# A gated spatial block behind linear attention: the written order of the work, who rounds ten pieces of W, and the unread products of the start

## The chip, the cores and the metric

The kernel runs on one core of a Trainium2 chip. The time is the device time of one execution in microseconds; of several executions the median counts. The profile shows one execution. The engines are TensorE (PE, with its weight loads PEld), VectorE (DVE), ScalarE (ACT), GpSimd (POOL) and SyncE (SP), which here only begins transfers.

## The reference

Linear attention with a product feature map, then a gated block whose gate mixes the positions:

```python
def phi(x):                                   # r = 8, so 64 features of 32 values
    a = np.einsum('rd,bhsd->bhsr', S1, x)
    b = np.einsum('rd,bhsd->bhsr', S2, x)
    return np.einsum('bhsi,bhsj->bhsij', a, b).reshape(*x.shape[:-1], r * r)
q_p, k_p = (phi(q), phi(k))                   # b, h, s, d = 4, 4, 1088, 32
kv = np.einsum('bhsf,bhsd->bhfd', k_p, v)
z = np.sum(k_p, axis=2)
num = np.einsum('bhsf,bhfd->bhsd', q_p, kv)
den = np.einsum('bhsf,bhf->bhs', q_p, z)[..., None] + 1e-06
x = num / den                                 # heads side by side: (4, 1088, 128)
h = np.maximum(x @ w_in, 0.0)                 # w_in (128, 1024)
u, v = (h[..., :512], h[..., 512:])
v_n = (v - mean(v)) / np.sqrt(var(v) + 1e-06)
v_s = np.einsum('ts,bsd->btd', w_spatial, v_n) + b_spatial[None, :, None]
return (u * v_s) @ w_out                      # w_out (512, 128)
```

S1, S2, w_in, w_out and w_spatial come as 64-bit or 32-bit numbers as they are drawn; the 64-bit ones are turned into 32-bit ones on the chip.

## The kernel before

Large products are made of three: each operand is split into a high part, rounded to the type fp32r, and a low part, the rest. `mm3` writes high x high, low x high and high x low into one bank. Small products of the attention (lines 759, 796, 845, 859, 873) use plain f32.

The names, with the batch as the first digit. `kab`, `qab`: projections of keys and queries with S1 and S2 (line 759); `ka`, `qa` copy one half out of the bank on ScalarE (764), `kp`, `qp` multiply the halves on VectorE (766). `kv0:1` to `kv0:3` sum keys x values (796); `kd0` masks that sum (822). `tq` turns the query features (845), `qpT` copies them (849), `nd` makes numerators and denominators (859), `x32` divides (866), `xt` turns x (873), `xh` and `xl` are its high and low parts (877, 878). `pv` is x times the second half of w_in (bank tag `sd`, two banks), in three pieces for each third of the positions; `vt` evicts it with relu (969), `st` and `mv` are its statistics (971, 972), `sd00` to `sd02` the square root (991), `t1`, `rs`, `nm` small steps behind it; `vt..:4` to `vt..:6` apply the norm (1007 on VectorE, 1010 on ScalarE), `vh` and `vl` are the parts of the result (1076, 1079). `pu` is the first half of w_in times x (bank `pu`, one bank), `u` its eviction (1127). `v9` holds rows of ones. `sp` are the products with W, w_spatial turned (1135 to 1146).

W comes in 9 rows of 128 positions (kt) and three column pieces c of 424, 332 and 332. `wt<kt><c>` is the load of a piece, `wTh` its rounding (line 732, on ScalarE), `wTl` its low part (736). The pieces c = 1 and 2 pass through seven buffers `pl`, those of c = 0 through `wl<kt>`. `wi_raw1`, `wi_raw0` and `wo_raw` are the halves of w_in and w_out as 64-bit numbers; `from_f64` turns them in seven steps (`wi_x1:1` to `wi_x1:7`, lines 655 to 668); `wih` and `wil` are the parts (672, 587).

The kernel is first recorded as a list of named operations and then laid out by `schedule`: a planner with costs for each operation. For batch 0 the list `ORDER` ranks all operations, and whichever engine is free takes the best-ranked operation that is ready by the planner's costs; for the rest the list `THEN` gives each engine's order. `FORCE` says on which engine some kinds run. An engine executes what it was given in that order and waits at the first instruction whose operands or buffer are not there. Where the planner sees TensorE idle it puts in products of zeros that nobody reads (`fill`, 64 columns, line 619); `small` makes groups of 32x32 products (606) at three places, and `N_WARM` = 5 warm products (600) stand at the start. A dummy square root on ScalarE, `eps:1` (line 625), is its first instruction.

Batch 0 has its attention alone in the head of the program, followed by pv and pu, and from then on the W products; the attentions of batches 1 to 3 lie among the main products of the batch ahead. In batch 3 the W products of part of the columns are made of sums of pieces (lines 1192 to 1385).

Of the kernel before, what the change touches and what calls it, by code (L numbers as in the profile page):

```python
# [70 lines left out]
ORDER = """  # L71
kt00:1 z9:1 eps:2 z9:2 s_raw:1 eps:1 v93:1 wps:1 v90:1 kt01:1 wps:2 v92:1 v91:1 wps:3 wi_raw1:1 wps:4
kt02:1 wps:5 qt00:1 wps:6 mask_sb:1 sk:1 sk:2 v00:1 sk:3 sk:4 b32:1 sk:5 sk:6 v01:1 sk:7 v02:1
kab00:1 kab01:1 ka00:1 kp00:1 ka01:1 kp01:1 ident_sb:1 wi_x1:1 qt01:1 wi_x1:2 kab02:1 wi_x1:3 ka02:1 wi_raw0:1 qab00:1 kp02:1
qt02:1 qa00:1 bh:1 kv0:1 wt10:1 wi_x1:4 wt70:1 kv0:2 qp00:1 wt00:1 wt50:1 kv0:3 wi_x1:5 wTl:10 tq00:1 bl:1
wi_x1:6 tq01:1 wt30:1 qpT00:1 qab01:1 kd0:1 qpT01:1 wi_x1:7 qa01:1 nd00:1 qp01:1 wih:1 wil:1 wt80:1 tq10:1 wi_x0:1
rec0:1 tq11:1 rec0:2 wt60:1 wi_x0:2 qab02:1 x320:1 qpT10:1 qpT11:1 qa02:1 wt40:1 wi_x0:3 wTh:2 xt0:1 qp02:1 nd01:1
xh0:1 wt01:1 wTh:8 xl0:1 wt11:1 wTh:1 wTl:2 pv000:1 rec1:1 wi_x0:4 wt21:1 wTh:6 pv001:1 wt20:1 rec1:2 vt00:1
wi_x0:5 wTl:11 tq20:1 x321:1 wTh:4 tq21:1 st000:1 vt00:2 wt31:1 xt1:1 qpT20:1 wi_x0:6 pv002:1 qpT21:1 wt41:1 wTl:6
wTh:9 nd02:1 wi_x0:7 xh0:2 wo_raw:1 wTh:7 xl0:2 wt51:1 wih:2 st001:1 pv010:1 wTh:10 rec2:1 vt00:3 wil:2 wTh:11  # L80
rec2:2 pv011:1 wTl:9 vt01:1 x322:1 qt10:1 qt11:1 pu000:1 wTh:12 qt12:1 vt01:2 st002:1 xt2:1 wt61:1 u000:1 st010:1
pv012:1 xh0:3 mv00:2 wTh:5 mv00:3 mv00:1 pu010:1 xl0:3 sd00:1 vt01:3 rs00:1 st011:1 pv020:1 u010:1 t100:1 wTh:3
st012:1 pv021:1 vt02:1 t100:2 mv01:2 pu020:1 rs00:2 mv01:1 vt02:2 nm00:1 mv01:3 vt00:4 pv022:1 sd01:1 u020:1 st020:1
vh00:1 pab10:1 st021:1 pu030:1 vt02:3 rs01:1 vl00:1 abT10:1 pab11:1 vt00:5 qd10:1 st022:1 pab12:1 wTh:16 sp000:1 qd10:2
mv02:1 t101:1 vh00:2 vt00:6 sp020:1 abT11:1 t101:2 sp010:1 vl00:2 vh00:3 qd11:1 sp030:1 mv02:2 wTh:14 rs01:2 sp000:2
mv02:3 qd11:2 nm01:1 vl00:3 wo_x:1 sp020:2 sp030:2 sd02:1 vt01:4 vt01:5 sp000:3 wTl:3 sp030:3 vh00:4 wo_x:2 sp010:2
vh00:5 vl00:4 sp020:3 sp010:3 wTh:13 rs02:1 wo_x:3 sp000:4 vt01:6 t102:1 vl00:5 sp010:4 wTh:15 sp030:4 t102:2 wTl:14
vh00:6 sp020:4 rs02:2 sp010:5 wo_x:4 wt71:1 abT12:1 sp030:5 qd12:1 nm02:1 vl00:6 sp020:5 vt02:4 sp000:5 qd12:2 vt02:5
sp000:6 vt02:6 vh00:7 sp030:6 vh00:8 sp010:6 vl00:7 sp020:6 vh00:9 vl00:8 sp030:7 v91:2 sp010:7 v92:2 vh00:10 wTh:17
sp030:8 v90:2 wTl:8 sp010:8 v93:2 sp000:7 wTl:1 sp030:9 sp000:8 wTl:5 sp020:7 wo_x:5 sp020:8 wTl:4 sp030:10 sp030:11  # L90
wo_x:6 sp030:12 sp020:9 sp020:10 wTl:13 sp020:11 kt10:1 sp020:12 wTl:7 sp010:9 kt11:1 sp010:10 sp010:11 wo_x:7 sp010:12 kt12:1
sp020:13 sp020:14 wTl:17 sp000:9 wt81:1 woh:1 sp000:10 sp000:11 wTl:16 wt02:1 sp000:12 sp000:13 wTl:15 sp000:14 wt12:1 sp000:15
wTl:12 sp000:16 wt22:1 sp000:17 wTl:18 sp000:18 sp010:13 wt32:1 wol:1 sp020:15 sp020:16 wt42:1 sp020:17 sp020:18 wTl:19 sp030:13
v10:1 sp030:14 u000:2 sp030:15 wt52:1 sp030:16 wTh:18 sp030:17 u020:2 kab10:1 g000:1 v11:1 wTl:20 wTh:19 v12:1 g000:2
wTh:20 wt62:1 sp001:1 wTl:21 ka10:1 kt20:1 wTh:21 sp001:2 ka11:1 u030:1 kt21:1 wTl:22 sp001:3 wTh:22 sp030:18 wt72:1
sp001:4 wTh:23 wTl:23 u030:2 pu001:1 wt82:1 sp001:5 wTl:25 u001:1 kt22:1 sp010:14 wTh:24 sp010:15 sp010:16 sp010:17 wTl:26
fa100:1 sp010:18 sp001:6 u010:2 sp011:1 fb100:2 wTl:24 g010:1 sp001:7 fb100:1 sp001:8 g010:2 sp001:9 fa101:1 sp011:2 u001:2
po00:1 gh001:1 po00:2 fb101:1 wTh:26 gl001:1 sp011:3 g020:1 sp011:4 wTh:27 g030:1 sp011:5
""".split()
# [1462 lines left out]
```

## Time and profile before

| | before |
|---|---|
| median of 3 executions | 324.55 us (324.24 to 326.92) |
| span of the profiled execution | 322.9 us |
| TensorE busy | 317.1 us, 98% |
| VectorE, ScalarE, GpSimd busy | 228.1, 165.2, 64.2 us |

The span goes from the first to the last instruction; 1.65 us of the median lie around it. Busy time of TensorE is from its records, whose ends are modelled, and unread products count in it. A row of the time order gives start, duration of the group, engine, line, operation, tiles and, in brackets, the idle time ahead of it and what ended that. A product of plain f32 makes two records, a transpose one.

### The profile page before, as it was taken

The numbers are of one execution on the slowest core, as the hardware profiler recorded it, in microseconds if no ns is written. First come the engines' busy times: TensorE is split into PE (matmuls) and PEld (weight loads), VectorE is DVE, ScalarE is ACT, GpSimd is POOL, SyncE is SP. The second block draws the span as 40 slices with busy tenths as digits, with TensorE's granted clock in tenths as the row PEclk, the third lists the DMA queues.
The fourth block names the chain that finished last, engine by engine and source line by source line (L and its number), as shares of the span: only waits on it lengthen the run. The fifth ranks groups of instructions, "written<-read, shape, count | busy, mean of one in ns | idle before, by whom it ended". The sixth has DMA issues, their size and how long they took to land.

```text
span 322.9 us, 6972 instructions
## 1 busy us (share of the span) xinstructions
PE 317.1 (98%) x2708; PEld 301.9 (93%) x2708; DVE 228.1 (71%) x512; ACT 165.2 (51%) x391; POOL 64.2 (20%) x81
## 2 busy tenths in 40 slices
PE   8999999999999999999999999999999999999995
PEld 7887998999999899999899999999999999999995
DVE  3999995647799972889875658896325688439382
ACT  3499935525774625566535567462414465416040
POOL 1000004557201035321004702250001321103000
PEclk9999999999999999999999999999999999999999
DMA  7874129563010375001044215001000421000001
GB/s 237 294 230 142 50 60 293 187 196 87 14 59 20 89 240 152 7 26 39 9 122 130 63 49 168 2 0 44 1 0 2 121 71 42 0 3 0 2 1 69
DMA packets 21549, 26.84 MB, mean 83 GB/s; under 512 B 2828, under 2 KB 21260, under 8 KB 21516
## 3 DMA queue, kind: packets, MB, share of 16 engines
q1 hardware_dynamic: 21516, 26.39, 26.4%
...
## 4 chain that ended last, share of the span: by engine, by line
PE 86%; ACT 6%; DVE 4%; DMA 1%; issue 1%
PE sp L1135 17%; PE sp L1137 14%; PE sp L1144 14%; PE sd L1369 4%; PE sp L1369 3%; PE sd L577 3%; PE sd L579 3%; PE sd L578 3%; PE pu L577 3%; PE po L577 2%; PE po L579 2%; PE po L578 2%; PE sp L1146 2%; PE pu L578 2%; PE pu L579 2%; ACT wTh L732 2%
## 5 line engine op out<-in xcount | busy, mean ns | idle before, releaser
L1135 PE MATMUL sp<-wTh,vh 128*128 128x332 f32 (+1 forms) x350 | 114.8, 328 | 0.0
L1137 PE MATMUL sp<-wTh,vl 128*128 128x332 f32 (+1 forms) x304 | 99.0, 326 | 0.0
L1135 PEld LDWEIGHTS sp<-wTh,vh 128*128 128x128 f32 x350 | 65.7, 188 | 2.1 <-issue 0.7
L1144 PE MATMUL sp<-wl,vh 128*128 128x332 f32 x192 | 59.8, 311 | 0.0
L1137 PEld LDWEIGHTS sp<-wTh,vl 128*128 128x128 f32 x304 | 57.1, 188 | 0.8
L1144 PE MATMUL sp<-wTl,vh 128*128 128x424 f32 x112 | 37.1, 349 | 0.0
L1144 PEld LDWEIGHTS sp<-wl,vh 128*128 128x128 f32 x192 | 36.0, 188 | 0.0
L672 ACT CAST g<-u 128x332 fp32r<-128x332 f32 (+1 forms) x41 | 19.8, 490 | 31.6 <-DVE u L1172 21.4
L587 DVE TENSOR_TENSOR g<-u,g 128x332 fp32r<-128x332 f32 (+1 forms) x41 | 23.4, 572 | 17.1 <-PE po L578 11.2
L1172 DVE TENSOR_TENSOR u<-sp,u 128x332 f32<-128x332 f32 (+1 forms) x43 | 22.4, 520 | 14.8 <-PE sp L1146 8.4
L945 DVE RECIPROCAL c<-c 128x384 f32<-128x384 f32 (+1 forms) x9 | 21.8, 2419 | 15.1 <-ACT c L943 15.1
L1127 ACT ACTIVATE u<-pu 128x332 f32<-128x332 f32 (+1 forms) x44 | 20.6, 468 | 20.8 <-PE pu L579 15.9
L1048 ACT CAST vh<-vt 128x384 fp32r<-128x384 f32 x36 | 17.4, 511 | 19.3 <-DVE vt L1007 10.7
L914 POOL TENSOR_TENSOR pl<-pl,pl 128x384 f32<-128x384 f32 (+1 forms) x18 | 17.9, 1005 | 42.1 <-DMA pl<-qd 41.7
L971 DVE BATCH_NORM_STATS2 st<-vt 128x6 f32<-128x512 f32 x36 | 24.0, 684 | 2.1 <-ACT vt L969 1.9
L969 ACT ACTIVATE vt<-sd 128x512 f32<-128x512 f32 x36 | 21.4, 604 | 7.3 <-PE sd L579 6.6
L590 POOL TENSOR_TENSOR r<-pl,r 128x384 fp32r<-128x384 f32 (+1 forms) x18 | 17.6, 984 | 34.5 <-ACT r L672 34.5
L1050 DVE TENSOR_TENSOR vl<-vt,vh 128x384 fp32r<-128x384 f32 (+1 forms) x36 | 18.4, 522 | 5.4 <-ACT vh L1048 5.2
L1144 PEld LDWEIGHTS sp<-wTl,vh 128*128 128x128 f32 x112 | 21.0, 188 | 0.1
L736 POOL TENSOR_TENSOR wl<-pl,wTh 128x332 fp32r<-128x332 f32 x8 | 7.0, 901 | 50.9 <-ACT wTh L732 50.9
L577 PE MATMUL pu<-xh,wih 128*128 128x332 f32 (+1 forms) x48 | 16.5, 345 | 0.3 <-ACT kp L1127 0.3
L1007 DVE TENSOR_SCALAR vt<-vt,mv,sm 128x512 f32<-128x512 f32 x32 | 16.4, 559 | 0.0
...
## 6 DMA issues: line engine op xcount, KB each, us to landing
...
```

Source lines behind the costliest of these rows:

```text
L577: nc.tensor.matmul(o, ah, bh, start=start, stop=False)
L578: nc.tensor.matmul(o, ah, bl, start=False, stop=False)
L579: nc.tensor.matmul(o, al, bh, start=False, stop=stop)
L587: return lambda: nc.vector.tensor_tensor(out=o(), in0=a(), in1=bb(), op=ALU.subtract)
L945: op("DVE", 135 + 6.3 * n, lambda x32=x32, n=n: nc.vector.reciprocal(out=x32[:, :n], in_=x32[:, :n]), w=[x32])
L969: op("ACT", c_act(512, True), lambda pv=pv, t=t: nc.scalar.activation(vt[:, t], pv.ap, AF.Relu), r=[pv], w=[(vt, t)])
L971: op("DVE", 690, lambda stats=stats, t=t: nc.vector.bn_stats(out=stats.ap, in_=vt[:, t]), r=[(vt, t)], w=[stats])
L1135: nc.tensor.matmul(sp[:, :cw], vh[:, kt], wTh[:, kt, cs], start=(kt == begin), stop=False)
L1137: nc.tensor.matmul(sp[:, :cw], vl[:, kt], wTh[:, kt, cs], start=False, stop=False)
L1144: nc.tensor.matmul(sp[:, :cw], vh[:, kt], w_lo(kt, c), start=False, stop=False)
L1172: op("DVE", c_dve(cw), lambda: nc.vector.tensor_tensor(out=u.ap, in0=sp[:, :cw], in1=u.ap, op=ALU.mult), r=[sp], w=[u], lead=LEAD[1])
L1369: nc.tensor.matmul(x[:, :cw], p, q, start=i == 0 and n == 0, stop=end and i == 3 and n == 2)
```

## The change

- `ORDER`, `THEN`, `FORCE` and the paces are replaced by one list `SEQ`, which names each of 1808 operations with its engine; each engine executes its names in that order. `schedule` only plays the lists through with costs, to choose buffers and to place the fills.
- `load_w` may have the high part rounded by a transfer from SBUF to SBUF that GpSimd begins (`wTh:n@POOL`, line 707 of the new file). The new program has ten of these.
- The last step of `from_f64` and the low parts of w_in and w_out may run on GpSimd. In the head these go from VectorE to GpSimd: wi_x1:7, wil:1, wi_x0:7, wil:2, three low parts of W and vl00:3; more do so later. Some norms go from VectorE to ScalarE, the first step of `from_f64` of wi_x1 and wo_x from ScalarE to VectorE.
- Eight warm products instead of five, no groups of small products, fills of 128 columns instead of 64, of which eight are in the program, all of them ahead of kab02.
- The order of the loads differs: wi_raw1 comes second. `eps:1` comes late in ScalarE's order.

```diff
-N_WARM = 5
-SMALL_AT = ("pv011:1", 22)
-SMALL_FILL = (12, 15)
-N_SMALL = 36
+N_WARM = 8
...
+s_raw:1@SP z9:1@DVE z9:2@DVE wi_raw1:1@SP v91:1@POOL wps:1@PE v90:1@POOL kt00:1@SP wps:2@PE wps:3@PE kt01:1@SP wps:4@PE v00:1@SP wps:5@PE mask_sb:1@SP
...
+    def schedule(self):
+        ops = self.ops
+        lists = {}
+        for x in SEQ:
+            name, e = x.split("@")
+            lists.setdefault(e, []).append(name)
...
-    def small(n=None, out=None):
-        out = out or wps
-        for i in range(n or N_SMALL):
-            q = 32 * (i % 4)
-            nc.tensor.matmul(out[q:q + 32, :32], z9[:, q:q + 32], z9[:, :32], start=True, stop=True, tile_position=(0, q))
-
-    op("PE", 1300, f4=True, fn=small, r=[z9], w=[wps], due=0)
...
-        filled.append(tag)
-        if len(filled) == SMALL_FILL[0]:
-            small(SMALL_FILL[1], homes[tag, slot])
-        else:
-            nc.tensor.matmul(homes[tag, slot][:, :64], z9.ap, z9[:, :64], start=True, stop=True)
+        nc.tensor.matmul(homes[tag, slot][:, :P], z9.ap, z9.ap, start=True, stop=True)
...
-        step(c1, lambda v: v.tensor_tensor(out=out() if out else x(), in0=x(), in1=ev(), op=ALU.add), [(x32, "e"), (x32, "x")], [w_out or (x32, "x")])
...
+        def add(v):
+            return lambda: v.tensor_tensor(out=out() if out else x(), in0=x(), in1=ev(), op=ALU.add)
+
+        op("DVE", c1, add(nc.vector), r=[(x32, "e"), (x32, "x")], w=[w_out or (x32, "x")], sh=True, alts=[("POOL", c_pool(n), add(nc.gpsimd))] if n > NSK else [])
...
-        op("ACT", c_act(cw), lambda: nc.scalar.copy(out=wTh[:, kt, cs], in_=raw[:, :cw]), r=[raw], w=[(wTh, (kt, c))])
+        cast = "POOL", C_SWD, lambda: nc.gpsimd.dma_start(out=wTh[:, kt, cs], in_=raw[:, :cw])
+        op("ACT", c_act(cw), lambda: nc.scalar.copy(out=wTh[:, kt, cs], in_=raw[:, :cw]), r=[raw], w=[(wTh, (kt, c))], kb=cw // 2, alts=[cast])
```

The start of TensorE's order before: warm and small products, a fill, two projections of keys, eight fills, the third projection, a projection of queries, the sums of keys and values.

```order
L600 MATMUL sd_161<-u_87 128x128 x5
L606 MATMUL sd_161<-u_87 32x32 x36
L619 MATMUL po_222<-u_87 128x64
L759 MATMUL sd_224<-sk,kt 64x2x32 x6
L759 MATMUL sd_161<-sk,kt 64x2x32 x6
L619 MATMUL po_222<-u_87 128x64 x8
L759 MATMUL sd_224<-sk,kt 64x2x32 x6
L759 MATMUL sd_161<-sk,c_124 64x2x32 x6
L619 MATMUL po_222<-u_87 128x64
L796 MATMUL pu_273<-v,kp_93 32x33 x24
L796 MATMUL pu_273<-v,kp_94 32x33 x24
L796 MATMUL pu_273<-v,kp_95 32x33 x24
```

And after, in the same place:

```order
L587 MATMUL sd_159<-u_87 128x128 x8
L592 MATMUL po_187<-u_87 128x128 x2
L735 MATMUL sd_190<-sk,kt 64x2x32 x6
L735 MATMUL sd_159<-sk,kt 64x2x32 x6
L592 MATMUL po_187<-u_87 128x128 x6
L735 MATMUL sd_190<-sk,kt 64x2x32 x6
L772 MATMUL pu_225<-v,kp_93 32x33 x24
L735 MATMUL sd_159<-sk,c_124 64x2x32 x6
L772 MATMUL pu_225<-v,kp_94 32x33 x24
L735 MATMUL sd_190<-sk,c_125 64x2x32 x6
L818 MATMUL po_187<-u_88,kp_93 128x128 x3
L818 MATMUL po_300<-u_88,kp_93 128x128 x3
L772 MATMUL pu_225<-v,kp_95 32x33 x24
```

The small products are gone, two of the fills come ahead of kab00 and six ahead of kab02, none comes behind, and the projections of queries stand between the sums.

ScalarE before, from the eviction vt00:3 (the first row, line 969) on; sd00 is the row of line 991.

```order
L969 ACTIVATE vt_92<-sd_224 128x512
L732 CAST wTh<-pl_148 128x332
L969 ACTIVATE vt_90<-sd_161 128x512
L732 CAST wTh<-pl_149 128x332
L969 ACTIVATE vt_90<-sd_224 128x512
L1127 ACTIVATE kp_93<-pu_273 128x424
L877 CAST xh_117<-sp_427 128x384
L732 CAST wTh<-wl_109 128x424
L991 ACTIVATE sm_71<-mv_80,eps 128x3
L969 ACTIVATE vt_90<-sd_161 128x512
L1127 ACTIVATE kp_94<-pu_273 128x424
```

And after, from vt00:3 to the xh of the last third:

```order
L937 ACTIVATE vt_92<-sd_190 128x512
L647 CAST wih<-v 128x512
L708 CAST wTh<-pl_148 128x332
L708 CAST wTh<-wl_109 128x424
L959 ACT_TABLE_LOAD
L959 ACTIVATE sm_71<-mv_80,eps 128x3
L937 ACTIVATE vt_90<-sd_159 128x512
L937 ACTIVATE vt_90<-sd_190 128x512
L708 CAST wTh<-wl_111 128x424
L850 CAST xh_117<-sp_376 128x384
L708 CAST wTh<-wl_101 128x424
L937 ACTIVATE vt_90<-sd_159 128x512
```

The square root has a table load ahead of it, and three of the evictions come behind it; there are fewer casts of W (line 732 before, 708 after) in between.

GpSimd before, behind its four casts at the start:

```order
L736 ISA
L736 TENSOR_TENSOR wl_782<-pl_145,wTh 128x332
L736 TENSOR_TENSOR wl_750<-pl_151,wTh 128x332
L736 TENSOR_TENSOR wl_678<-pl_150,wTh 128x332
L736 TENSOR_TENSOR wl_772<-pl_146,wTh 128x332
```

And after, from the first operation behind two of these casts:

```order
L641 TENSOR_TENSOR vt_91<-vt_91 128x512
L602 CAST v_137<-u_87 64x128
L602 CAST v_138<-u_87 64x128
L577 TENSOR_TENSOR wil<-vt_91,wih 128x512
L707 DMA wTh<-wl_103 128x424
L641 TENSOR_TENSOR v<-v 128x512
L712 TENSOR_TENSOR wTl_106<-wl_107,wTh 128x424
L577 TENSOR_TENSOR wil<-v,wih 128x512
L712 TENSOR_TENSOR wl_464<-pl_148,wTh 128x332
L707 DMA wTh<-wl_105 128x424
L707 DMA wTh<-pl_149 128x332
```

Before, low parts of the third column piece of W are all that stands there; after, the two halves of w_in (lines 641 and 577), the first transfers (707) and low parts of the first piece stand ahead.

## Rows read from the trace of the kernel before

**Rows 1.** The page: span, busy time of each engine, the chain by engine.

```profile
span 322.9 us, 6972 instructions
...
PE 317.1 (98%) x2708; PEld 301.9 (93%) x2708; DVE 228.1 (71%) x512; ACT 165.2 (51%) x391; POOL 64.2 (20%) x81
...
PE 86%; ACT 6%; DVE 4%; DMA 1%; issue 1%
```

**Rows 2.** Windows: us, busy time and count by engine, PEclk, DMA share, GB/s.

```profile
0.00:5.00 5.00, 3.68 (x83) 3.39 (x83) 1.68 (x10) 1.49 (x2) 1.21 (x8) 1.00 0.55 146
5.00:18.20 13.20, 12.58 (x307) 11.57 (x308) 11.27 (x23) 6.42 (x18) 0.00 (x0) 1.00 0.92 312
18.20:32.10 13.90, 13.90 (x122) 10.60 (x121) 13.82 (x40) 13.68 (x33) 0.00 (x0) 1.00 0.55 176
...
54.60:318.80 264.20, 264.01 (x2050) 254.76 (x2051) 180.67 (x391) 129.39 (x306) 61.66 (x72) 1.00 0.20 62
```

**Rows 3.** All waits of TensorE: us in total, times, longest.

```profile
PE sd L600 <- DVE u L596: 1.3, 1, 1.3
PE po L845 <- DVE kp L766: 0.6, 1, 0.6
PE pu L577 <- ACT kp L1127: 0.3, 1, 0.3
```

**Rows 4.** TensorE in order of time, 0 to 40 us.

```profile
1.32 2.50 PE L600 MATMUL sd<-u 128*128 128x128 f32 x10 [1.32 <-DVE u L596]
3.75 1.19 PE L606 MATMUL sd<-u 128*32 128x32 f32 x72
...
5.49 1.30 PE L759 MATMUL sd<-sk,kt 128*64 128x64 f32 x24
6.72 2.00 PE L619 MATMUL po<-u 128*128 128x64 f32 x16
8.65 0.57 PE L759 MATMUL sd<-sk,kt 128*64 128x64 f32 x12
...
12.02 0.88 PE L845 MATMUL po<-u,kp 128*128 128x128 f32 x6 [0.62 <-DVE kp L766]
...
13.59 1.50 PE L859 MATMUL sp<-u,c 128*128 128x66 f32 x12
...
18.21 0.48 PE L577 MATMUL sd<-wih,xh 128*128 128x512 f32 x1
...
19.68 0.82 PE L845 MATMUL po<-u,kp 128*128 128x128 f32 x6
...
23.61 0.60 PE L606 MATMUL po<-u 128*32 128x32 f32 x44
...
25.82 0.48 PE L577 MATMUL sd<-wih,xh 128*128 128x512 f32 x1
```

**Rows 5.** VectorE in order of time, 3 to 20 us.

```profile
10.41 0.68 DVE L661 SCALAR_TENSOR_TENSOR vt<-vt,vt 128x512 uint32<-128x512 uint32 x1
11.01 0.95 DVE L766 TENSOR_TENSOR kp<-ka,sd 128x768 f32<-128x768 f32 x1
...
14.61 0.69 DVE L587 TENSOR_TENSOR wil<-vt,wih 128x512 fp32r<-128x512 f32 x1
```

**Rows 6.** ScalarE in order of time, 0 to 35 us.

```profile
0.73 1.28 ACT L625 ACT_TABLE_LOAD   x1 [0.73 <-PEq L1550]
...
17.53 1.44 ACT L732 CAST wTh<-wl 128x424 fp32r<-128x424 f32 x3
```

**Rows 7.** GpSimd by line: count, busy us, mean ns.

```profile
L736 POOL TENSOR_TENSOR wl<-pl,wTh 128x332 fp32r<-128x332 f32 x8 | 7.0, 901 | 50.9 <-ACT wTh L732 50.9
```

**Rows 8.** The chain that ended last, in order of time.

```profile
31.45 0.71 ACT vt L1010
...
47.21 4.58 DMA pl<-in_wT
```

**Rows 9.** VectorE in order of time, 119 to 121.5 us.

```profile
120.45 1.45 DVE L587 TENSOR_TENSOR g<-u,g 128x424 fp32r<-128x424 f32 x1 [0.61 <-ACT g L672]
```

More of the change, by code (lines that the diff above doesn't have):

```diff
@@ L73 @@
[L73 to L92, printed above, removed]
@@ new lines @@
+kab02:1@PE kv0:1@PE ka02:1@ACT wi_raw0:1@SP wi_x1:5@DVE qab00:1@PE kp02:1@DVE wt10:1@SP qa00:1@ACT kv0:2@PE wt80:1@SP qp00:1@DVE qab01:1@PE qa01:1@ACT
+wi_x1:6@DVE bh:1@ACT tq00:1@PE tq01:1@PE qp01:1@DVE qpT00:1@ACT wi_x1:7@POOL kv0:3@PE qpT01:1@ACT qab02:1@PE kd0:1@DVE nd00:1@PE qa02:1@ACT wt01:1@SP
+v92:1@POOL wih:1@ACT qp02:1@DVE v93:1@POOL wt30:1@SP wi_x0:1@ACT wil:1@POOL wt11:1@SP tq10:1@PE rec0:1@DVE wt50:1@SP tq11:1@PE rec0:2@DVE x320:1@DVE
+qpT10:1@ACT wt20:1@SP tq20:1@PE qpT11:1@ACT wTh:2@POOL wi_x0:2@DVE wt40:1@SP xt0:1@PE nd01:1@PE wi_x0:3@DVE wt70:1@SP xh0:1@ACT wi_x0:4@DVE wt21:1@SP
@@ new lines @@
+wt31:1@SP xl0:1@DVE tq21:1@PE wt60:1@SP rec1:1@DVE wi_x0:5@DVE pv000:1@PE rec1:2@DVE wt41:1@SP x321:1@DVE qpT20:1@ACT wTh:9@ACT qpT21:1@ACT wTh:4@ACT
+pv001:1@PE wi_x0:6@DVE vt00:1@ACT wt00:1@SP xt1:1@PE st000:1@DVE wt51:1@SP wi_x0:7@POOL pv002:1@PE xh0:2@ACT vt00:2@ACT xl0:2@DVE nd02:1@PE
+wo_raw:1@SP vt00:3@ACT wTl:4@POOL st001:1@DVE wih:2@ACT st002:1@DVE wTh:11@ACT pv010:1@PE wil:2@POOL rec2:1@DVE wTh:5@ACT mv00:2@DVE rec2:2@DVE
+mv00:3@DVE mv00:1@DVE x322:1@DVE pv011:1@PE sd00:1@ACT vt01:1@ACT rs00:1@DVE wTl:2@DVE pu000:1@PE vt01:2@ACT t100:1@DVE st010:1@DVE wTl:13@POOL
@@ L248 @@
 class Op:
-    __slots__ = ("n", "name", "eng", "fn", "occ", "dur", "deps", "succ", "due", "left", "ready", "first", "tiles", "start", "end", "chosen", "alts", "kb", "rw", "stretch", "sh", "after", "f4")
+    __slots__ = ("n", "name", "eng", "fn", "deps", "succ", "left", "first", "tiles", "start", "end", "alts", "kb", "sh", "after", "f4")
 class Fill:
@@ new lines, in schedule @@
+            for e, os in lists.items():
+                if at[e] == len(os) or os[at[e]].left:
+                    continue
+                o = os[at[e]]
+                s = max([free[e], o.after, *(d.end + (-165 if d.eng == e == "PE" else self.LAT.get((d.eng, e), 35)) for d in o.deps)])
+                if e == "POOL":
+                    s = max(s, shared_to - 40)
+                need = {}
+                for t in o.first:
+                    if t.slot is None:
+                        need.setdefault(t.tag, []).append(t)
+                ok = True
+                for tag, ts in need.items():
+                    n = len(ts)
+                    if n > len(slots[tag]) or [t.n for t in ts] != list(range(taken[tag], taken[tag] + n)):
+                        ok = False
+                        break
+                    s = max(s, slots[tag][n - 1][0])
+                if ok and (best is None or s < best[0]):
+                    best = (s, e, o)
@@ L411, in schedule @@
                     order += [Fill(lambda home=home: self.fill(*home))] * n
[L412 to L418 removed]
+            o.start = s
             for t in o.first:
```

500 lines of the change are left out of this document (222 added, 278 removed).

## The prediction

> **What bounds the kernel now.** I read the page first. TensorE is busy for 317.1 us of a span of 322.9 us, and 86% of the chain that ended last is its own work [rows 1]. So the end moves only if TensorE gets less to do, does it in less time, or waits less. The windows show where that could be [rows 2]: from 54.6 to 318.8 us it is busy for 264.01 of 264.20 us, which leaves 0.19 us. All of its idle time that an operand ends is three waits, 1.3, 0.6 and 0.3 us [rows 3]; the first is the start of the program.
>
> The busy share hides one thing. In the first 24 us TensorE also runs products that nobody reads, and these are waiting time under another name. In time order [rows 4]: 2.50 us of warm products and 1.19 us of small ones before the first keys at 5.49, sixteen records of them at 6.72 that last until the next keys at 8.65, and 0.60 us of small ones at 23.61, in front of pv011. (Three pieces of 0.43 to 0.45 us between 9.5 and 16.6 us are not shown.) From kab00 on they come to 1.93 + 0.60 + three times some 0.44 = 3.85 us; with the waits of 0.6 and 0.3 us the head could give back 4.75 us at most.
>
> What sets the pace there are the other engines. From 5.0 to 18.2 us VectorE is busy for 11.27 of 13.20 us; from 18.2 to 32.1 us VectorE has 13.82 and ScalarE 13.68 of 13.90 us [rows 2]. TensorE's 13.90 of 13.90 us there is no proof that it sets the pace, since it holds small products and pipelined ends. All the gain to be had lies before some 55 us.
>
> **The early gaps.** Eight warm products take the place of five and of the 36 small ones. A warm product is two records; ten took 2.50 us, the next work starting 2.43 us after the first, so eight take 8 x 0.49 = 3.9 us and end at 5.2 us (before: warm and small ended at 4.94). Two of the new 128-column products follow. One of 64 columns took 0.24 us at 6.72 (1.93 us for eight, two records each); six transposes of 128 columns at 19.68 took 0.82 us, 0.14 us a record, so two records of the new width are 0.27 us. I take 0.24; by the warm ones it would be 0.49, and kab02 below would come 2 us later. kab00 can start at 5.7 us, against 5.49. Its data no longer lead the queue: 512 KB of wi_raw1 stand ahead of them. By 5.0 us 146 GB/s had brought 730 KB [rows 2], and s_raw, wi_raw1 and kt00 are 768 KB, so the load is late by 0.1 to 0.5 us at most against 5.2 us and TensorE would not get there sooner anyhow. Two projections (1.3 us) and six fills (1.45 us) put kab02 at 8.4 us, against 8.65: 0.2 us, hardly a gain.
>
> The gain comes behind it, on VectorE. Now a step of from_f64 (started 0.60 us ahead) stands between kp02 and qp00 [rows 5]; with wi_raw1 early it is done before, so qp00 starts 0.2 + 0.60 = 0.8 us earlier, and what follows from it in a line (tq00, now at 12.02 after the wait of 0.62 us, then kd0 and, at 13.59, nd00) does too. kd0 has one step of from_f64 and the second qp ahead of it on VectorE, 0.68 + 0.95 us; that takes qp00's end at 11.15 to 12.8 us and leaves 0.2 to 0.8 us for nd00. Between nd00 and pv000 stood wi_x1:7 and wil:1, some 0.69 us each, both of which go to GpSimd, so the shorter gain grows again. I take 0.8 us at pv000 (18.21 before, 17.4 now); bounds 0.2 and 1.4.
>
> **From pv000 to the W products.** TensorE loses work in this stretch: tq20 and tq21 (0.82 us) now lie before pv000, and the 0.60 us of small products are gone. By TensorE alone pv022 ends 0.8 + 0.8 + 0.6 = 2.2 us earlier. By ScalarE it is less. Up to the last of the nine evictions (vt) it has six casts of W to do in place of twelve: 6 x 0.48 = 2.9 us less [rows 6]. Against that stand one ACT_TABLE_LOAD of 1.28 us and up to two norms of 0.71 us each [rows 8], which VectorE did before. The balance is between 1.6 us less and 0.2 us more, 0.7 us less in the middle; with the earlier start that is 0.8 + 0.7 = 1.5 us. The smaller of the two counts, so **1.5 us**, bounds 0.6 and 2.2.
>
> The table load has to be placed. Before, the dummy square root is ScalarE's first instruction and its load lies at 0.73 us, where nothing waits. Now that dummy comes after 75 rows, and the load that the square root needs stands in front of sd00, with the evictions vt01:1 and vt01:2 queued behind it. These free the two banks which pv012 and pv020 write; in between TensorE has pu000, xt2 and the product before, some 1.6 us by the distance from the end of the small products at 24.21 to pv012 at 25.82 [rows 4]. The wait is thus partly covered; uncovered it is 1.3 us, and my 1.5 us becomes 0.6.
> The load's 1.28 us [rows 6] agree with 1283 ns in the Trainium skill, "ScalarE: Activation LUTs", section "What ACT_TABLE_LOAD costs"; that page adds a drain of some 1.38 us to each switch, which no row here shows, since nothing ran ahead of the load. By it the sum would be worse by up to 1.4 us.
>
> **wil:2 on GpSimd.** pu000 reads it as the third of its three products. wi_x0:7, wih:2, one low part of W and wil:2 follow each other there. GpSimd did 332 columns in 901 ns [rows 7], so 512 columns are 1.4 us if that grows in proportion, against 0.69 us on VectorE [rows 5]. The two operations cost 1.4 us more in a row, but VectorE is freed of some 2.7 us ahead of wi_x0:6. I take 0; bounds 0 and 0.7 us.
>
> **The transfers that GpSimd begins.** The built program has ten of them, not eleven. Eight of them stand in GpSimd's list ahead of the second round of v92, in the stretch that ends at some 50 us. Each takes a cast of 0.48 us from ScalarE, and I have no row of a transfer that GpSimd begins. The nearest is the load of a W slice by SP, which ScalarE waited 4.58 us for [rows 8]; that was mostly a wait for its buffer and for the transfers ahead. The low part of W has to wait for such a transfer, on VectorE in most cases. I take 0, because wTh:2 comes right behind wil:1, near 15 us, and the first W product stands at 32; bounds -0.3 and +4.6 us. The casts behind it ended in TensorE's last wait of 0.3 us [rows 3]; the order there is another, and I count **0.3 us** gained, bounds 0 and 0.3.
>
> **Behind 55 us.** TensorE has the same products to do in another order: 0 for that, +-0.3. VectorE and GpSimd get more in common. Where a two-input VectorE operation meets GpSimd's, it took 1.45 us for 424 columns [rows 9], where 512 columns had taken 0.69: at least 0.76 us more. GpSimd's rows grow from 86 to 138. VectorE idles for 83 of the 264 us, so most of this is absorbed; I take +0.3 us, bounds 0 and 2.
>
> **The sum.** -1.5 - 0.3 + 0.3 = -1.5 us on a profiled span of 322.9 us, so 321.4 us. The median is 324.55, with 1.65 us around the span; these stay. Forecast: **323.0 us**. Its own range, from 2.2 + 0.3 gained to the cover of the table load gone and the low bounds elsewhere, is 321.5 to 325.0.
>
> **The rivals.**
> *The head gives back nearly all of it.* If VectorE and ScalarE, freed of some 4 us each, let TensorE run through, most of the 4.75 us go: 4 of them make 320.5 us. For it: the two engines are full in just this stretch. Against it: the eight unread products at 6.7 us wait for keys that now come later, and these 1.9 us stay. It decides where pv000 starts before 16.5 us. Faster by over 1% is below 321.3 us, about what a measurement of this kernel can tell from no change. Chance 0.25.
>
> *GpSimd becomes late.* Up to 50 us it gets five operations of 512 columns at 1.4 us, three low parts at 0.9 to 1.15 us and eight transfers. If each of these has to wait for a VectorE operation to end (VectorE is 85 to 99% busy in the two windows before 32 us), it runs at the pace of collisions as in [rows 9], double its own: 10.2 us of operations become 20, and the transfers queue behind them. wil:2 would then come 2 us late, and the last high parts of W's second columns some 3 us after their products are due; TensorE's list is fixed, so it has nothing to do in their place. 2 + 3 - 1.5 = +3.5 us: **328.0 us**, slower. It decides when wTh:10 lands after 50 us. Against it: VectorE's operations from PSUM or in place are many, and GpSimd sat idle to 53 us.
> A rule speaks for this rival: the Trainium skill, "SBUF — State Buffer", section "Who interferes with whom", has a transfer begun by GpSimd starved of its descriptors while VectorE runs in a two-port mode, and names another queue as the cure. No row of before shows such a transfer. Chance 0.11.
>
> *The clock.* All small products and all fills behind kab02 are gone. The granted clock reads 1.00 in every window [rows 2], the 2.4 GHz level; still the first products, after idleness, took 0.24 us a record where the transposes of that width at 19.68 took 0.14. If the level fell to 1.2 GHz between 9 and 18 us, the products on the path there (three projections, four transposes, nd00, xt0: some 4.5 us) would take that again: 323.0 + 4.5 = 327.5. It decides if PEclk reads below 1.00 there. Against it: TensorE has real work in most of that time. Chance 0.05.
>
> *Nothing comes through.* TensorE's work from 18 us on is the bound and the new orders only move waits: 324.5 us. It shares the band with the forecast; the two hold 0.59.
>
> **How the numbers follow.** Faster 0.27 (the first rival and the forecast's lower edge), same 0.59, slower 0.14 (GpSimd 0.11, part of the clock). Below 320.3 and above 327.3 lie some 0.1 each, so the range is 320.3 to 327.3.
>
> **What the profile after would show.** kab02 near 8.4, nd00 near 13, pv000 at 17.0 to 18; no unread product after 9 us; a load of 1.28 us on ScalarE near 22 us, and behind it a wait of TensorE on vt01 below 1.3 us; the first W product (32.10 before) at 30.6; no wait of 0.3 us near 54; TensorE waits below 0.5 us behind. I am wrong if TensorE waits for GpSimd's parts, if the W products start after 32 us, or if the gain at 32 us is lost between 32 and 55 us.

## The result

The new kernel takes **328.79 us** (median of 4, 327.85 to 329.62) against 324.39 (4 runs): ratio 1.0137, interval 1.0103 to 1.0172. It is slower by 1.4%, clear of the noise; the forecast was 323.0 us, and the range ended at 327.3. The profiled span is 327.0 us, 4.1 more than before (322.9), so the loss is inside the span. Medians count every execution; ratios leave out those in a slow state, over 1.5% above the fastest of their kernel.

The page after, its head and the row of the granted clock ([rows 1] before):

```profile
span 327.0 us, 6708 instructions
...
PE 318.4 (97%) x2562; PEld 302.4 (92%) x2562; DVE 218.6 (67%) x470; ACT 164.4 (50%) x382; POOL 105.2 (32%) x133
...
PEclk9999899999999999999999999999999999999999
```

TensorE's work is nearly the same; the span is longer by waits and, in this execution, by a slice in which the clock reads 8. GpSimd's busy time rises from 64.2 to 105.2 us, VectorE's falls by 9.5 us, ScalarE's hardly.

TensorE's waits (total, times, longest; [rows 3] before):

```profile
PE sd L566 <- ACT vt L937: 2.3, 2, 1.8
...
PE pu L772 <- issue: 0.6, 1, 0.6
PE sd L566 <- ACT xh L850: 0.3, 1, 0.3
PE po L818 <- DVE kp L742: 0.3, 1, 0.3
```

Windows, columns as in [rows 2]:

```profile
18.20:32.10 13.90, 11.24 (x58) 8.55 (x58) 12.62 (x33) 11.78 (x25) 7.14 (x8) 0.96 0.72 230
32.10:54.60 22.50, 22.50 (x119) 20.63 (x118) 17.79 (x46) 14.38 (x30) 7.69 (x11) 0.95 0.39 106
54.60:318.80 264.20, 263.94 (x2080) 254.44 (x2079) 173.05 (x357) 130.60 (x311) 85.71 (x103) 1.00 0.23 68
```

Where before TensorE had no idle time from 18.2 to 32.1 us, it now has 2.66, and PEclk is below 1.00 there and in the next window. From 54.6 us on nothing is lost: TensorE idles there for 0.26 us, before for 0.19. To say where the 4 us arise, I counted at which time TensorE had begun the same number of columns of products that are read in the two traces (warm products, small ones and fills left out, 666,432 columns in all; the order differs, so single points can mislead by some 0.5 us). The last column is an experiment further down:

```
columns begun   before, us   after minus before   both edits minus before
     18,000         21.0            +0.3                  +0.3
     24,000         25.7            -0.5                  -0.5
     27,000         27.2            +1.0                  -0.2
     29,000         27.9            +3.3                  +0.8
     30,000         28.4            +3.7                  +0.8
     33,000         30.1            +4.8                  +0.9
     47,000         36.9            +4.5                  +1.5
     90,000         57.2            +3.4                  +0.4
    660,000        316.0            +4.0                  +0.9
```

At 25.7 us the new kernel is 0.5 us ahead (the small products at 23.61 are gone), and then more than 5 us are lost by 30 us. TensorE in order of time there and ahead of it ([rows 4] before):

```profile
8.96 0.57 PE L735 MATMUL sd<-sk,kt 128*64 128x64 f32 x12
...
11.91 0.87 PE L818 MATMUL po<-u,kp 128*128 128x128 f32 x6 [0.27 <-DVE kp L742]
...
13.72 0.39 PE L772 MATMUL pu<-v,kp 128*32 128x33 f32 x21 [0.56 <-issue]
...
14.60 1.52 PE L832 MATMUL sp<-u,c 128*128 128x66 f32 x12
...
19.17 0.48 PE L566 MATMUL sd<-wih,xh 128*128 128x512 f32 x1
...
26.10 0.51 PE L566 MATMUL sd<-wih,xh 128*128 128x512 f32 x1 [0.53 <-ACT vt L937]
...
27.41 0.50 PE L566 MATMUL sd<-wih,xh 128*128 128x512 f32 x1 [0.33 <-ACT xh L850]
...
31.13 0.80 PE L566 MATMUL sd<-wih,xh 128*128 128x512 f32 x1 [1.80 <-ACT vt L937]
...
34.66 0.36 PE L1096 MATMUL sp<-wTh,vh 128*128 128x424 f32 x1
```

ScalarE in the same stretch:

```profile
23.39 0.57 ACT L708 CAST wTh<-wl 128x424 fp32r<-128x424 f32 x1
23.98 1.28 ACT L959 ACT_TABLE_LOAD   x1
25.27 0.30 ACT L959 ACTIVATE sm<-mv,eps 128x3 f32<-128x3 f32 x1
25.48 1.06 ACT L937 ACTIVATE vt<-sd 128x512 f32<-128x512 f32 x2
...
29.79 0.81 ACT L978 ACTIVATE vt<-vt,sm,sm 128x512 f32<-128x512 f32 x1 [1.49 <-DVE sm L966]
30.51 0.58 ACT L937 ACTIVATE vt<-sd 128x512 f32<-128x512 f32 x1
```

VectorE, and GpSimd, from 27 us on:

```profile
27.46 0.15 DVE L966 SCALAR_TENSOR_TENSOR sm<-sm,sm 128x3 f32<-128x3 f32 x1
...
27.99 1.50 DVE L966 SCALAR_TENSOR_TENSOR sm<-sm,sm 128x3 f32<-128x3 f32 x1
```

```profile
27.82 0.53 POOL L707 DMA_DIRECT2D wTh<-pl  x1
28.36 1.10 POOL L712 TENSOR_TENSOR wTl<-wl,wTh 128x424 fp32r<-128x424 f32 x1
```

Read from the wait of 1.80 us backwards. pv022 starts at 31.13 because the eviction at 30.51 (vt02:1) frees its bank late. That eviction stands behind the norm vt00:5 in ScalarE's list, and ScalarE sat idle for 1.49 us ahead of that norm, until VectorE had made the scale it reads. That last small step, 128x3 elements, normally 0.15 us (27.46), took 1.50 us. It ends with GpSimd's low part of W (28.36 to 29.46). Its row begins 0.37 us ahead of GpSimd's, whose times are rough, so these rows alone do not tell what held it; the experiment low_later does. The whole line is late besides by the table load at 23.98, in front of the square root that starts it. And the granted clock:

```profile
30.00:31.00 1.00, 0.00 (x0) 0.00 (x0) 1.00 (x3) 1.00 (x3) 0.00 (x0) 1.00 0.56 158
31.00:32.00 1.00, 0.87 (x2) 0.77 (x3) 1.00 (x4) 1.00 (x4) 0.00 (x0) 0.55 0.09 20
32.00:33.00 1.00, 1.00 (x4) 0.35 (x5) 0.64 (x4) 0.96 (x4) 0.00 (x0) 0.50 0.09 16
...
34.00:35.00 1.00, 1.00 (x5) 0.95 (x5) 0.96 (x4) 0.91 (x4) 0.00 (x0) 0.74 0.00 0
35.00:36.00 1.00, 1.00 (x8) 0.98 (x6) 1.00 (x3) 1.00 (x3) 0.02 (x1) 1.00 0.22 34
```

After the idle stretch from 29.3 to 31.1 us the clock is at its lower level, 1.2 GHz, until 34.5 us; the products there take nearly twice as long (those of 512 columns follow each other by 0.43 us in place of 0.23). Not every execution has this: the mean granted clock is 0.995 in two of the four (328.82 and 329.62 us) and 1.000 in the others (327.85 and 328.76). So most of the loss is there without the lower clock, which by these four costs some 0.9 us where it comes.

### The profile page after: what moved, and what is told of

It is laid out like the page before. It is cut to its first block, busy times and chain, and to the rows that moved or that the text cites. A ratio compares the mean times of both kernels' runs of the same rounds, so it can differ in the third digit from the quotient of the medians.

```text
span 327.0 us, 6708 instructions
## 1 busy us (share of the span) xinstructions
PE 318.4 (97%) x2562; PEld 302.4 (92%) x2562; DVE 218.6 (67%) x470; ACT 164.4 (50%) x382; POOL 105.2 (32%) x133
## 4 chain that ended last, share of the span: by engine, by line
PE 93%; DVE 3%; ACT 2%; issue 0%; ACTq 0%
PE sp L1096 18%; PE sp L1098 15%; PE sp L1105 15%; PE sd L1327 4%; PE sp L1327 3%; PE sd L566 3%; PE sd L568 3%; PE sd L567 3%; PE pu L566 3%; PE pu L567 2%; PE pu L568 2%; PE po L566 2%; PE po L567 2%; PE po L568 2%; PE sp L1107 2%; PE sd L735 2%
## 5 line engine op out<-in xcount | busy, mean ns | idle before, releaser
L574 DVE TENSOR_TENSOR g<-u,g 128x332 fp32r<-128x332 f32 (+1 forms) x41 | 26.5, 647 | 11.0 <-PE po L567 7.1
L885 POOL TENSOR_TENSOR pl<-pl,pl 128x384 f32<-128x384 f32 (+1 forms) x18 | 19.0, 1062 | 44.3 <-DMA pl<-qd 39.9
L937 ACT ACTIVATE vt<-sd 128x512 f32<-128x512 f32 x36 | 21.0, 597 | 17.8 <-PE sd L568 17.5
L1010 ACT CAST vh<-vt 128x384 fp32r<-128x384 f32 x36 | 17.8, 510 | 1.5 <-DVE vt L975 1.5
L566 PE MATMUL sd<-wih,xh 128*128 128x512 f32 x36 | 15.2, 422 | 2.7 <-ACT vt L937 2.3
L1012 DVE TENSOR_TENSOR vl<-vt,vh 128x384 fp32r<-128x384 f32 (+1 forms) x24 | 15.6, 662 | 3.2 <-ACT vh L1010 3.2
L742 DVE TENSOR_TENSOR kp<-ka,sd 128x768 f32<-128x768 f32 x15 | 14.0, 950 | 4.9 <-ACT ka L740 4.2
```

Of the source, the lines that this page charges most:

```text
L566: nc.tensor.matmul(o, ah, bh, start=start, stop=False)
L574: return lambda: nc.vector.tensor_tensor(out=o(), in0=a(), in1=bb(), op=ALU.subtract)
L937: op("ACT", c_act(512, True), lambda pv=pv, t=t: nc.scalar.activation(vt[:, t], pv.ap, AF.Relu), r=[pv], w=[(vt, t)])
```

## The experiments

Each changes the new kernel, unless it says otherwise. Ratios are to the kernel before, run beside it on the same chip; the new kernel's is 1.0137. The theories, by their letters in the expectations: **L**, the late table load starts the loss; **H**, VectorE's small step, held by GpSimd's operation, holds the norm, and the norm the evictions behind it; **G**, the transfers that GpSimd begins cost the time; **C**, part of the loss is the clock behind the wait. In the edits of `SEQ` other than load_early and norm_later, the bound up to which the planner may place fills (`FILL_TO`) went from 50 us to 12 as well (9.5 in four_fixed_sum_early); the traces show the same eight fills as the new kernel, all ahead of kab02.

**load_early.** `eps:1@ACT` moves in `SEQ`:

```diff
-z9:1@DVE z9:2@DVE wi_raw1:1@SP
+z9:1@DVE z9:2@DVE eps:1@ACT wi_raw1:1@SP
```

> The new kernel with the dummy square root at the head of ScalarE's list again, so that its only table load lies at 0.7 us. Theory L (the load of 1.28 us ahead of sd00 starts the loss of 3.7 us between 27 and 39 us): the waits of TensorE of 0.5 and 1.8 us before pv012 and pv022 shrink to under 0.5 us together, the clock stays at its upper level, time 325.5 us or less. Rival H (the norm of vt00 on ScalarE, which waits for a small step that VectorE cannot finish while GpSimd makes a low part, holds the evictions up): only the wait of 0.5 us goes, the one of 1.8 us stays above 1 us, time 327.5 to 328.5. Rival G (the transfers that GpSimd begins): no change, 328.8.

328.15 us, 1.0114 (1.0077 to 1.0151). The profiled execution (326.44 us) has the wait on vt in one piece:

```profile
PE sd L566 <- ACT vt L937: 1.8, 1, 1.8
```

The waits of 0.5 and 0.3 us are gone, the one of 1.8 us stays, as H had said. The interval overlaps that of the new kernel; by the time alone this edit is not told from nothing. The clock sets this execution apart. TensorE has the same wait of 1.80 us here, to 29.98, and behind it PEclk stays at 1.00:

```profile
30.00:31.00 1.00, 0.96 (x5) 0.48 (x5) 1.00 (x4) 1.00 (x3) 0.00 (x0) 1.00 0.00 0
```

The other five executions have a mean clock of 0.995 and take 327.53 to 328.94 us. So such a wait does not always bring the lower level, and the times of this edit have to be read beside their clock: at 1.000 it takes 326.44 us where the new kernel takes 327.85 and 328.76, at 0.995 a median of 328.24 where that takes 328.82 and 329.62.

**before_load_late.** The kernel *before*, one word changed:

```diff
-nc.scalar.activation(eps[:1, 1:], z9[:1, :1], AF.Sqrt)
+nc.scalar.activation(eps[:1, 1:], z9[:1, :1], AF.Relu)
```

> The kernel before with relu in the dummy activation in place of the square root (it writes a number that nobody reads): one table load more on ScalarE, ahead of sd00 at 27 us, and no other instruction changed on any engine. Theory L: ScalarE is full there and TensorE waits on its evictions, so 1.0 to 1.3 us slower than before or more, 325.5 to 326. Rivals H and G: ScalarE's queue has slack of a microsecond by the full banks, slower by under 0.5 us.

325.83 us, 1.0043 (1.0013 to 1.0074): 1.4 us slower by the ratio. Its ScalarE and its new wait of TensorE:

```profile
27.18 1.28 ACT L991 ACT_TABLE_LOAD   x1
28.48 0.30 ACT L991 ACTIVATE sm<-mv,eps 128x3 f32<-128x3 f32 x1
```

```profile
PE sd L577 <- ACT vt L969: 1.2, 1, 1.2
```

One instruction of 1.28 us on ScalarE became 1.24 us of TensorE's waiting. That settles its price in the kernel before: all of it, as theory L had expected.

**low_later.** One low part on GpSimd goes behind vl00:3, off the small steps:

```diff
-wTl:5@POOL
...
 vl00:3@POOL
+wTl:5@POOL
```

> The new kernel with one low part of W (wTl:5) on GpSimd put behind vl00:3, so that no operation of GpSimd lies beside the small steps of VectorE at 28 us. Theory L: the small step takes 0.16 us in place of 1.5, and the norm behind it starts at 28.5 in place of 29.8 us; the wait of 1.8 us falls by some 1.2, but what the load costs stays: 326.5 to 327.5. Rival H: 325.5 or less, with the clock at its upper level. Rival G: no change.

327.30 us, 1.0091 (1.0059 to 1.0123). VectorE in that place:

```profile
26.98 0.15 DVE L966 SCALAR_TENSOR_TENSOR sm<-sm,sm 128x3 f32<-128x3 f32 x1
...
27.51 0.15 DVE L966 SCALAR_TENSOR_TENSOR sm<-sm,sm 128x3 f32<-128x3 f32 x1
```

```profile
29.30 0.50 PE L566 MATMUL sd<-wih,xh 128*128 128x512 f32 x1 [0.45 <-ACT vt L937]
```

The last small step takes 0.15 us with GpSimd's operation gone, though a transfer is being begun by GpSimd beside it. That shows what held it. TensorE's wait before pv022 falls from 1.80 to 0.45 us, and the clock holds, in all seven executions (0.998 or more). The time is what theory L had expected (326.5 to 327.5), not H's 325.5; its interval still overlaps that of the new kernel.

**load_early_low_later.** Both edits.

> The new kernel with both edits: the table load at the head again and wTl:5 behind vl00:3 on GpSimd. Theories L and H together (the load costs some 1.3 us, the held small step some 1.4 us with what the clock does behind a wait of 1.8 us): TensorE waits under 0.5 us between 24 and 32 us, the products with W start below 31 us, time 324 to 326. If each edit alone had only moved the same wait (one cause, two names), no better than the better of the two alone, 327.3. Rival G: the loss that stays, 327 or more, is that of the transfers.

325.86 us, 1.0057 (1.0030 to 1.0083), clear of the new kernel's interval: 2.9 of 4.4 us come back. The two are different causes that add, and the waits show it: each edit alone took its own and left the other's. In the table of columns both edits stand at +0.9 at 30.1 us, where the new kernel stands at +4.8.

**norm_later.** `vt00:5@ACT` goes behind `vt02:2@ACT`.

> The new kernel with the norm vt00:5 on ScalarE put behind the evictions vt02:1 and vt02:2. Rival H: the evictions no longer wait for the small step, TensorE's wait of 1.8 us before pv022 goes, the clock holds, 325.5 us or less (unless vh00:2, one step later, is then what the first products wait for). Theory L: 0 to 1 us gained, 327.5 to 328.8, with a wait of 1.3 us left somewhere. Rival G: no change.

329.51 us, 1.0156 (1.0118 to 1.0194). A miss for H in this form: TensorE waited 1.57 us in front of another product (line 870) and the clock fell all the same (0.993 to 0.995 in five of six executions). Moving the blocked instruction back leaves others behind it late; the held step is what has to go.

**keep_busy.** Eight unread products of 512 columns stand in the wait:

```diff
             s, e, o = best
+            order += [Fill(lambda: self.keep())] * 8 if o.name == "pv022:1" else []
...
+    def keep():
+        nc.tensor.matmul(homes["po", 0][:, :], wih[:, DH:DH + P], wih[:, DH:], start=True, stop=True)
```

> The new kernel with eight unread products of 512 columns of wih with itself put ahead of pv022, in the wait of 1.8 us. Theory C (behind that wait the granted clock drops to its lower level for 3.4 us, which costs some 1.6 us): the clock holds, first product with W at some 33.1 in place of 34.7 us, 327.2. Without the clock's part (the wait alone costs the time): 328.8 to 329.2.

327.81 us, 1.0095 (1.0064 to 1.0126). The windows:

```profile
30.00:31.00 1.00, 1.00 (x5) 0.51 (x5) 1.00 (x3) 1.00 (x3) 0.00 (x0) 1.00 0.64 178
31.00:32.00 1.00, 0.97 (x5) 0.48 (x7) 1.00 (x3) 1.00 (x3) 0.00 (x0) 1.00 0.09 16
32.00:33.00 1.00, 1.00 (x7) 0.71 (x8) 0.64 (x4) 0.96 (x3) 0.00 (x0) 1.00 0.00 0
```

```profile
33.05 0.35 PE L1102 MATMUL sp<-wTh,vh 128*128 128x424 f32 x1
```

The clock holds and the first product with W starts at 33.05 in place of 34.66 us. Of these 1.6 us, 1.4 lie behind pv022, where the clock had fallen (2.16 us from its start to that product in place of 3.53); over all executions of the two programs it is 1.0 us by the medians, with intervals that overlap. The rest of the loss is the wait itself.

**casts_back.** The ten `wTh:n@POOL` become `@ACT` in place.

> The new kernel with its ten high parts of W rounded by ScalarE again, at the same places of the list, and nothing else moved. Rival G (the transfers cost time: 2.2 us to landing, and a half us of GpSimd each): faster by 1 us or more, under 327.8. Theories L and H: ScalarE gets six casts of 0.48 us back ahead of and between the evictions it is late with, so slower by 0.5 to 3 us, 329.3 to 332.

328.80 us, 1.0132 (1.0104 to 1.0160): no change, which neither expectation had named. In sum the transfers neither cost nor gain. It is a sum, though: with them gone GpSimd's low part comes earlier, at 27.07 us, and holds the small step before (0.93 us), the clock stays up in the profiled execution, and TensorE waits in five pieces of 0.33 to 0.76 us. In the new kernel the transfers land late and harmlessly:

```profile
wTh<-pl POOLq DMA_DIRECT2D x7, 166.0 KB, 2.2
```

2.2 us from issue to landing (the first of the ten 5.3), some 0.55 us of GpSimd each; no engine's wait ended with one.

**no_fills.** `FILL_TO` = 0: the eight warm products stay, the eight fills go.

> The new kernel without the eight fills ahead of kab02 (the eight warm products stay). If the fills only sit in waiting time: kab02 starts when its data are there, VectorE's chain is the bound, pv000 0 to 0.9 us earlier, 328 to 328.8. If TensorE needs them to have its upper clock level in the head: the granted clock falls below 1.00 before 15 us, pv000 later, 329 to 333.

331.30 us, 1.0183 (1.0142 to 1.0224).

```profile
6.00:7.00 1.00, 0.42 (x13) 0.33 (x12) 0.96 (x3) 0.24 (x1) 0.00 (x0) 1.00 1.06 359
7.00:8.00 1.00, 0.37 (x11) 0.23 (x8) 1.00 (x2) 0.24 (x1) 0.00 (x0) 0.77 1.06 372
8.00:9.00 1.00, 1.00 (x32) 0.88 (x36) 1.00 (x2) 0.17 (x1) 0.00 (x0) 0.50 0.93 276
```

TensorE was busy for 0.42 and 0.37 us of these two microseconds, and the clock went to its lower level; it did so twice more in this execution, from 17.8 and from 34.9 us on. kab02 started 1.1 us earlier and all of that was lost, to the clock and to a stop of 2.52 us in kv0:3, of which more below. In two of the six executions the clock stayed at 1.000 without the fills; these take 328.86 and 329.24 us. So the fills keep the clock up in most executions, and where it stays up without them nothing is gained.

**four_fixed, four_fixed_casts_back.** load_early, wTl:5 behind wTh:10, and vt00:5 behind vt02:1; then the same with the casts back.

> The new kernel with the table load at the head, wTl:5 on GpSimd behind its last transfer of that stretch (wTh:10), and the norm vt00:5 on ScalarE behind the eviction vt02:1. Theories L and H: the waits of 0.5 us before pv022 and of 0.6 us on vl near 38 us that were left with two edits go too; some 1 us under the 325.9 of the two edits, 324.5 to 325, about the kernel before. If the rest of the loss is not in these waits: 325.5 to 326.5.

> The kernel with the three edits, and all ten high parts of W back on ScalarE. This prices the transfers with the other causes away. If they help as ScalarE's relief: slower by 1 to 2.5 us, since ScalarE has six casts of 0.48 us more before the last eviction. If they neither help nor harm, as with the causes still there: within 0.7 us.

326.61 (1.0071, 1.0049 to 1.0094) and 327.07 us (1.0079, 1.0052 to 1.0107). The first is a miss: the third edit brought nothing; in its new place wTl:5 holds another small step (36.74 us) for 1.43 us. That transfers matter with the other causes away is not seen either.

**low_on_vector, all_low_on_vector.** load_early, and wTl:4, wTl:13, wTl:5 and vl00:3 on VectorE; then also both ends of `from_f64` and both low parts of w_in.

> The new kernel with the table load at the head, and the four operations of GpSimd between pv and the W products that read two inputs of SBUF (wTl:4, wTl:13, wTl:5, vl00:3) on VectorE at the same places of its list. If a small step held by GpSimd is worse than the work itself (1.35 us against 4 x 0.6 us in all): the waits of 1.8 us before pv022 and 0.6 us on vl near 38 us are gone, 324.5 to 325.7. If VectorE is too full there for 2.4 us more: TensorE waits for xl or for the statistics, 326.5 or more.

> The same, with the last steps of from_f64 and the low parts of w_in (wi_x1:7, wil:1, wi_x0:7, wil:2) on VectorE too, so that GpSimd does nothing in the head but begin transfers. If the relief of VectorE ahead of pv000 is worth anything: 0.5 to 2 us slower than the other. If kd0 and nd00 wait for TensorE's stop near 13 us anyhow: within 0.5 us of it.

327.08 (1.0076, 1.0044 to 1.0108) and 328.21 us (1.0108, 1.0071 to 1.0146). In the first no VectorE operation ahead of 60 us takes longer than its kind, and still it is no better than load_early_low_later: VectorE is full from 18.2 to 32.1 us (13.76 of 13.90), and TensorE waits 0.4 us on xl and 0.3 on xh. So this is no way back; that GpSimd's share of the work relieves VectorE by about what it costs is argued from this one time. The second has a stop of 1.2 us near 13 us and the lower clock from 16 to 19 us in its profiled execution; in the four with a clock of 0.999 or more it takes 326.95 to 328.28 us, 1.0 us more than the first by their medians at such a clock. That is within the expected 0.5 to 2, but the two intervals overlap.

**four_fixed_sum_early.** four_fixed, with `kv0:3@PE` behind `qab01:1@PE`.

> The same, with the last sum of keys and values (kv0:3) ahead of the turns of the first query features, where the kernel before has it. If its place is why nd00 came at 14.6 us and not at 13: kd0 no longer waits 1.2 us for it, nd00 0.6 to 0.9 us earlier, the whole 0.5 us faster. If the stop of 0.6 to 0.9 us in its middle, which no operand ends, comes at its own time: the stop moves to another place, nd00 stays within 0.3 us, and so does the time.

327.14 us, 1.0075 (1.0050 to 1.0099).

```profile
13.63 0.33 PE L772 MATMUL pu<-v,kp 128*32 128x33 f32 x15 [1.92 <-issue]
```

```profile
14.00:15.00 1.00, 1.00 (x16) 0.83 (x18) 0.30 (x1) 0.53 (x2) 0.13 (x1) 1.00 1.01 353
15.00:16.00 1.00, 1.00 (x14) 0.93 (x10) 0.42 (x1) 1.00 (x4) 0.00 (x0) 0.63 0.83 164
16.00:17.00 1.00, 1.00 (x7) 1.00 (x6) 0.54 (x1) 0.64 (x2) 0.79 (x1) 0.50 0.90 308
```

The stop inside kv0:3 came all the same, now 1.92 us long, to 13.63 us (13.14 in four_fixed), and nd00 came 1.2 us later, at 15.19; both expectations missed that. It is not the place of the sum. Behind the stop the clock fell, which makes this the slowest of the profiled spans but one (329.1 us); the five executions with a clock of 0.998 or more take 326.3 to 327.4 us, no less than four_fixed.

**load_pause, q_load_later.** load_early_low_later; in the first, SP's list has a transfer that must wait for ScalarE ahead of wi_raw0, in the second qt02 comes behind wi_raw0.

> The kernel with the two edits (early table load, one low part later), and the small transfer of the bias's high part, which needs a cast of ScalarE at some 11.8 us, put ahead of the load of wi_raw0 in SP's list, so that all later loads wait for it. If TensorE's stop in the middle of kv0:3 (0.3 to 2.5 us, to some 13 us, ended by no operand) is a wait for its own instructions behind the loads: no stop over 0.2 us in the trace, kd0 before 13 us. If it has nothing to do with the loads: the stop is there with 0.3 us or more. The time may suffer in either case from wi_raw0 coming 1.5 us late: 325 to 328.

> The kernel with the two edits, and the load of qt02 behind that of wi_raw0, as in the kernel before, so that the loads ahead of the wait for wi_raw0's buffer are 192 KB less and the pause there comes earlier. If the stop of TensorE comes from loads in its way: shorter or gone, 325 to 325.7. If not: as without this edit, 325.9.

326.49 (1.0097, 1.0061 to 1.0133) and 328.25 us (1.0121, 1.0078 to 1.0164); both are spread over more than 4 us, and their slowest have the lowest clocks (two of seven and three of six at 0.994 or less). In the trace of the first the stop is gone:

```profile
10.00:11.00 1.00, 1.00 (x60) 0.82 (x56) 0.90 (x2) 0.22 (x1) 0.00 (x0) 1.00 0.00 2
11.00:12.00 1.00, 0.73 (x6) 0.64 (x6) 1.00 (x3) 0.49 (x3) 0.04 (x1) 1.00 0.00 0
12.00:13.00 1.00, 1.00 (x62) 0.89 (x60) 0.78 (x2) 0.71 (x2) 1.00 (x1) 1.00 0.04 3
```

The loads stand still from 10 to 13 us (the last but one column is the DMA share), and among TensorE's waits there is none that no operand ends; in the second it is 0.2 us, but there TensorE waits 0.9 us for the load that was moved. low_on_vector has no such wait either, without an edit of the loads.

Two further readings of the traces tell what the stop is. First, its place: in all 13 profiles that have it, exactly 221 records of TensorE's products lie ahead of it. In no_fills, where 16 records of fills are gone, it comes 16 records deeper in kv0:3 (43 of its 48 done, in the new kernel 27); in four_fixed_sum_early, where the sum stands earlier, at 33. So it is bound to a place in TensorE's own instructions and not to an operation. Second, the trace's queue of instructions (q8 on the page) has one packet of 16,384 bytes in flight just ahead, and the stop ends 0.7 to 1.5 us after the packet does, early or late (packets end between 11.55 and 14.35 us). In the new kernel the packet took 1.80 us, to 12.58; in load_pause, with the loads at rest, 0.91 us, to 10.77, while record 221 came at 12.3; in low_on_vector it ended at 11.22, and 0.17 us between two starts are left of the stop at that place. So the stop has a fixed place and follows that packet; that the packet holds TensorE's own instructions is inferred from this. That the loads delay it fits, but load_pause is the only trace that takes the loads away, and it stays argued.

## Why the prediction was wrong

**The early gaps.** kab02 at 8.4 us was forecast, 8.96 came. The two fills ahead of kab00 took 1.0 us in place of 0.48, the bound I had named and not taken, but the warm products had ended early, so kab00 was late by only 0.17 us (5.87); the two projections took 1.55 us in place of 1.3, and the six fills 1.54 in place of 1.45. That the load of the keys would not count held in this trace; in ten of the 14 variants TensorE waits 0.2 to 0.9 us for it. The step of from_f64 between kp02 and qp00 was gone, as forecast, but qp00 now waited for its projection, which stands behind the late kab02 and kv0:1 (10.02 us, before 9.05), and tq00 came at 11.91, 0.1 us earlier than before. Then nd00 at 14.60 in place of 13: kv0:3 stopped for 0.56 us and kd0 waits for it. I had not seen that this sum moved behind tq00 and tq01. pv000 came at 19.17, not 17.4. Of the 0.8 us, nothing.

**From pv000 to the W products: the step that failed.** "The smaller of the two counts, so 1.5 us" sized ScalarE by a balance of its work. In that balance the norms stood at 0.71 us each, and what they wait for at nothing. ScalarE's busy time did fall, to 11.78 of 13.90 us, and it still was late, because it stood idle for 1.49 us behind its own list. A sum of work says nothing about an engine that executes in order: what counts was the one norm ahead of an eviction, and what that norm waits for. In place of 0.7 us gained in this stretch (1.5 with the head), 4.5 were lost (from +0.3 at 21 us of the kernel before to +4.8 at 30).

**The table load** I had placed rightly (near 22 us forecast, 23.98 came, a wait of 0.53 us on vt behind it, below 1.3), and I had named its full price as a bound. It costs 1.4 us in the kernel before, and once the held step is away the same again: 327.30 against 325.86 us, 1.4 by the medians and 1.1 by the ratios. "Partly covered" was wrong.
The drain of 1.38 us that the Trainium skill adds to each switch of tables ("ScalarE: Activation LUTs", "What ACT_TABLE_LOAD costs") does not show: the cast ahead ended at 23.96, the load began at 23.98 and the square root at 25.27.

**Behind 55 us** I put +0.3 us for collisions of GpSimd and VectorE and 0.76 us for each. The mechanism was right, its place wrong: one collision, at 28 us, on a step of 0.15 us that I had not counted because it is small, held VectorE for 1.35 us, and TensorE for as much. Behind 55 us no more was lost than such points can tell: TensorE idles there for 0.26 us, and the difference is +4.5 us at 37, +3.4 at 57 and +4.0 at 316. The 0.3 us near 54 us came: that wait is gone.
The Trainium skill, "SBUF — State Buffer", "Who interferes with whom", has a VectorE instruction with two inputs from SBUF contend with a GpSimd instruction that reads SBUF; the 1.50 us against 0.15 us with GpSimd's operation moved agree. Its rule on starved transfers, for which the rival spoke, shows in no wait: nothing waited for a transfer, not even for the first, which took 5.3 us to land.

**The rivals.** The head gave nothing back: pv000 came at 19.17, not before 16.5. GpSimd was not late: wTh:10 landed at 41.5 us, before the 50 I had named, and the transfers were harmless in sum (casts_back). The clock did fall in two of four executions, not at 9 to 18 us where I had put it but behind the wait at 31, for 0.9 to 1.4 us; I had it as a cause and it was a consequence. In no_fills and four_fixed_sum_early it fell where the rival had it, or partly so.

**What stays open.** Some 1.6 us between both edits and the kernel before. The clock is not it: it reads 0.998 or more in eleven of the twelve executions. The profiled span with both edits is 1.0 us longer than before (323.9 against 322.9 us), and it has waits that the kernel before has not: 0.5 us before pv022, 0.6 on vl near 37 us, 0.6 on the loads of the keys and the stop of 0.9 near 13; how much of the 1.6 each of them makes was not taken apart. No version here beats the kernel before.
